# The head of a forward-and-backward kernel: skewed emission, queued loads, and w_down turned by transposing loads

## The chip, the core and the metric

The kernel runs on one core of a Trainium2 chip. The metric is device time in microseconds (us) for one execution. Five engines work side by side and meet through semaphores: PE (TensorE, matmuls and transposes into PSUM), DVE (VectorE), ACT (ScalarE), POOL (GpSimd) and SP (SyncE, which here only issues DMAs). Each engine takes its own instructions strictly in order, and so does each DMA queue. What waits at the front of a queue holds everything behind it.

## The reference

A block of a conditioned network is computed forward, and then the gradients of its output with respect to eight inputs. Cut to what matters (S = 2048 tokens, D = 576, F = 4608, bfloat16 inputs):

```python
mod = (silu(c) @ w_mod).reshape(1, 6, 1, D)            # sa, ca, ga, sb, cb, gb
h = layernorm(x) * (1 + ca) + sa
y = irfft2(rfft2(h) * (w_r + 1j * w_i))                # along tokens and features
x1 = x + ga * y
h2 = layernorm(x1) * (1 + cb) + sb
out = x1 + gb * (((h2 @ w_gate) * (h2 @ w_up)) @ w_down)
# and the gradients with respect to x, w_r, w_i, w_gate, w_up, w_down, c, w_mod, for a given grad_out
```

## The kernel before

The Fourier transforms are matmuls with tables of cosines and sines. The 2048 tokens stand as 16 tiles of 128 (token index `16 p + t`), the 289 frequencies of the feature axis as 73 groups of four. The program has three parts: the **head** (forward transform, filter, inverse transform, second normalisation, and the first backward product), the **main loop** over 36 blocks of 128 columns of F, and the **tail** (backward transform, remaining gradients, output). The change is in the head; the word "late head" is used below for its last stretch.

The head is written as plain loops, one after the other:

- **Modulation.** `mod_load(j)` brings a 576x576 piece of `w_mod` into `wm`, `mod_make(j, wm)` multiplies it (line 219, PSUM tile `modps`) and stores the result `modh[j]` to HBM from POOL's queue (line 224). Three are made ahead of stage 1, the other three after it.
- **Stage 1**, 16 steps (lines 250 to 280), one per token tile: normalise (`n`, `nm`, `hpp`), five TensorE transposes (`trp`), evacuation `hT` on ACT, column transform of ten matmuls (`zp` with the table `T_RD`), evacuation `zt`, row transform of four matmuls (`vp` with `T_G`), evacuation into `VA`.
- **Stage 2**, 19 steps (lines 292 to 332), one per 16 frequencies: transposes of `VA` (`trv`), evacuation `VT` on ACT, four matmuls with `T_BD` (`xp`), evacuation `Xc` (half on ACT, half on DVE) and its store to `xn_d`, six DVE products with the filter `wn` (`fm`, `Yg`), transposes (`try_`), `YT` on DVE, four matmuls with `T_BDA` (`ap_`), two evacuations on ACT back into `VA`.
- **Stage 3**, 16 steps (lines 341 to 384): inverse row transform (`upa`, `upb`, evacuated to `ut`), inverse column transform (`yp`, evacuated to `yb`); every second step the residual `x`, second normalisation and `h2p`, every fourth step a transposing DMA of `h2p` into `h2T`.
- **The first backward product** (lines 387 to 417), called the `ghh` work here: `grad_out` times `gb` is transposed on PE into `goT` (line 392). Then, for 18 pairs of 128-row blocks of `w_down`: a load of the pair (`wdn`), ten TensorE transposes (line 405), evacuations into `wdT` (576 on the partitions in five pieces, the fifth 64 wide), 40 matmuls (line 415, 20 per block) with `wdT` as weights, evacuations into `ghh_st` on ACT and DVE in turn, and per block a 512 KB store to `ghhT_d`.

A scheduler sets the final order: it takes the instructions by their place in the source where they are ready by its own estimate, and fills the engines with later ones where they are not. So the `ghh` work, last in the source of the head, is spread over stages 1 to 3, and what is left of it follows stage 3. PSUM of the head: five banks (`fps`) for stages 1 to 3, three (`u4ps`) for the `ghh` work. All loads and most stores are issued by SP and stand in one queue; `mod_make`'s stores, the stores of `n`, `y`, `x1` and part of the main loop's DMAs go through POOL. `wdT` and `wdn` have two buffers, each holding a pair of blocks.

The main loop (lines 462 to 516) begins with `gup` (line 492), which needs all of `h2T`, and goes on with `u8p` (lines 508 and 509) and `u57p` (line 445).

Of the kernel before, what the change touches and what calls it, by code (L numbers as in the profile page):

```python
# [10 lines left out]
BF = mybir.dt.bfloat16  # L11
# [8 lines left out]
NT = 16  # L20
S = 2048
D = 576
# [56 lines left out]
def build(ctx, tc, A_x, A_w_r, A_w_i, B_w_gate, B_w_up, B_w_down, c_in, w_mod, grad_out,  # L79
# [81 lines left out]
    with ExitStack() as hs:  # L161
# [52 lines left out]
        def mod_make(j, wm):  # L214
            for h in range(2):
                ps = fps.tile([128, 512], FP32, name="modps", tag="fp")
                for m in range(5):
                    K = KD[m]
                    nc.tensor.matmul(ps[:, 0:288], lhsT=sc_rep[0:K, m, :], rhs=wm[0:K, m, h * 288:(h + 1) * 288], start=(m == 0), stop=(m == 4))
# [24 lines left out]
        x_load(2)  # L244
        T["BD2"] = load_table(hp1, "BD2")
        T["BDA"] = load_table(hp1, "BDA")
# [3 lines left out]
        for t in range(NT):  # L250
            c4, tt = t // 4, t % 4
            if tt == 0:
                if c4 == 1:
                    x_load(3)
                xt = xts[c4]
                n1 = hw2.tile([128, 4, D], BF, name="n1")
                nmr1 = norm_stats(xt, hw2, 4, "ln1", rstd1g[:, t:t + 4])
            nc.scalar.activation(out=n1[:, tt, :], in_=xt[:, tt, :], func=ACT.Identity, bias=nmr1[:, tt:tt + 1], scale=rstd1g[:, t:t + 1])
# [9 lines left out]
            hT = hw2.tile([128, 5, 128], BF, name="hT")  # L268
            evac(hT[:], pt[:], eng="a")
            zt = hw2.tile([128, 2, FP], BF, name="zt")  # L270
            for cc in range(2):
                zp = fps.tile([128, 512], FP32, name="zp", tag="fp")
                for m in range(5):
                    nc.tensor.matmul(zp[:, :FP], lhsT=hT[:, m, :], rhs=T["RD"][:, m, cc, :], start=(m == 0), stop=(m == 4))
                evac(zt[:, cc, :], zp[:, :FP], eng=("a" if cc == 0 else "v"))
            for cc in range(2):
# [4 lines left out]

        nc.gpsimd.memset(wn[:, :, :, DF:FP], 0.0)
        nc.sync.dma_start(wn[:, 0, :, 0:DF], wr_v)
        nc.sync.dma_start(wn[:, 1, :, 0:DF], wi_v)
        for j in (MGA, MSB, MCB):
            mod_make(j, mod_load(j))
        r1.close()
        with ExitStack() as rc:  # L290
            c2 = pool("hc2", 2, "right", stack=rc)
            for ci in range(NCH):
                g0 = 4 * ci
                ng = min(4, NG - g0)
                f0, w = 4 * g0, 4 * ng
# [3 lines left out]
                VT = c2.tile([128, 4, 128], BF, name="VT")  # L299
                evac(VT[:, 0:ng, :], pt[:, 0:ng, :], eng="a")  # L300
                xp = fps.tile([128, 4, 128], FP32, name="xp", tag="fp")
                for j in range(ng):
                    nc.tensor.matmul(xp[:, j, :], lhsT=VT[:, j, :], rhs=T["BD2"][:], start=True, stop=True)
# [13 lines left out]
                Yg = c2.tile([128, 4, 128], BF, name="Yg")  # L317
# [3 lines left out]
                nc.vector.tensor_tensor(out=Ygv[:, :, :, 1, :], in0=mv_[:, 2], in1=mv_[:, 3], op=ADD)  # L321
                pt2 = fps.tile([128, 4, 128], BF, name="try_", tag="fp")
                for j in range(ng):
                    nc.tensor.transpose(pt2[:, j, :], Yg[:, j, :], ident[:])
                YT = c2.tile([128, 4, 128], BF, name="YT")
                evac(YT[:, 0:ng, :], pt2[:, 0:ng, :], eng="v")
                ap_ = fps.tile([128, 4, 128], FP32, name="ap_", tag="fp")
                for j in range(ng):
                    nc.tensor.matmul(ap_[:, j, :], lhsT=YT[:, j, :], rhs=T["BDA"][:], start=True, stop=True)
# [11 lines left out]
        for sa in range(NT):  # L341
            if sa % 2 == 0:
                xc = hw2.tile([128, 2, D], BF, name="xc")
                nc.sync.dma_start(xc[:], x_v[:, sa:sa + 2, :])
                x1 = hw2.tile([128, 2, D], BF, name="x1")
                yb = hw2.tile([128, 2, D], BF, name="yb")
                n2 = hw2.tile([128, 2, D], BF, name="n2")
            ut = hw2.tile([128, 3, 256], BF, name="ut", bufs=3)
# [9 lines left out]
            evac(ut[0:36, 2, :], upb[0:36, 0, :], eng="v")  # L358
            for h in range(2):
# [8 lines left out]
            if sa % 2 == 1:  # L368
                s0 = sa - 1
                nc.gpsimd.dma_start(y_d[:, s0:s0 + 2, :], yb[:])  # L370
                for i in range(2):
                    nc.vector.tensor_tensor(out=x1[:, i, :], in0=yb[:, i, :], in1=modh[MGA][:], op=MUL)
                    nc.vector.tensor_tensor(out=x1[:, i, :], in0=x1[:, i, :], in1=xc[:, i, :], op=ADD)
                nc.gpsimd.dma_start(x1_d[:, s0:s0 + 2, :], x1[:])
                nmr2 = norm_stats(x1, hw2, 2, "ln2", rstd2g[:, s0:s0 + 2])
                for i in range(2):
                    nc.scalar.activation(out=n2[:, i, :], in_=x1[:, i, :], func=ACT.Identity, bias=nmr2[:, i:i + 1], scale=rstd2g[:, s0 + i:s0 + i + 1])
                    nm = hw2.tile([128, D], BF, name="nm")
                    nc.vector.tensor_tensor(out=nm[:], in0=n2[:, i, :], in1=modh[MCB][:], op=MUL)
                    nc.vector.tensor_tensor(out=h2p[:, s0 + i, 0:D], in0=nm[:], in1=modh[MSB][:], op=ADD)  # L380
                nc.gpsimd.dma_start(n2_d[:, s0:s0 + 2, :], n2[:])
                if sa % 4 == 3:
                    s0 = sa - 3
                    nc.sync.dma_start_transpose(out=h2T[:, s0:s0 + 4, :, :].rearrange("q t m p -> q (t m) p"), in_=h2p[:, s0:s0 + 4, :].rearrange("p t d -> p (t d)"))
# [11 lines left out]
        for fb0 in range(0, NFB, FB4):  # L396
            nfb = min(FB4, NFB - fb0)
# [10 lines left out]
            for j in range(nfb):  # L408
                fb = fb0 + j
                st = u4w.tile([128, NT, 128], BF, name="ghh_st")  # L410
# [8 lines left out]
    with ExitStack() as ms:  # L419
# [3 lines left out]
        with ExitStack() as bs:  # L423
            FBW = 2
            FBT = 4
            wp = bs.enter_context(tc.tile_pool(name="wp", bufs=2))
            wtp = bs.enter_context(tc.tile_pool(name="wtp", bufs=2))
            ghp = bs.enter_context(tc.tile_pool(name="ghp", bufs=2))
            tp = bs.enter_context(tc.tile_pool(name="tp", bufs=2))
            tp2 = bs.enter_context(tc.tile_pool(name="tp2", bufs=2))  # L430
            sfp = bs.enter_context(tc.tile_pool(name="sfp", bufs=2))
            stg = bs.enter_context(tc.tile_pool(name="stg", bufs=4))
            wot = bs.enter_context(tc.tile_pool(name="wot", bufs=3))
            gups = bs.enter_context(tc.tile_pool(name="gups", bufs=3, space=PSUM))
            u8ps = bs.enter_context(tc.tile_pool(name="u8ps", bufs=3, space=PSUM))
            u57ps = bs.enter_context(tc.tile_pool(name="u57ps", bufs=2, space=PSUM))
# [450 lines left out]
```

## Time and profile before

| | |
|---|---|
| time, three runs | 1861.98 us median (1861.71 to 1865.2) |
| the profiled execution | 1858.56 us, of which the span of instructions is 1856.8 us |
| TensorE clock granted, mean over the span | 0.963 |
| busy: PE, DVE, ACT, POOL | 91%, 59%, 35%, 11% of the span |
| stage 1 begins (first `zp`) | 31.48 us |
| stage 2 begins (first `trv`) | 102.63 us |
| stage 3 begins (first `upa`) | 237.87 us |
| stage 3's last `yp`, late head begins | 298.93 us |
| first `u8p`: the main loop runs | 420.70 us |
| main loop gives way to the tail | about 1490 us |

The shares of the whole span are means over parts with different limits, so they are to be read stage by stage. Times are those of one profiled execution, counted from the start of its span. PE's busy time includes modelled ends of matmuls: two matmuls that follow each other closely overlap in it, and a stage in which PE is "85% busy" can still have gaps. For DMAs, SP's rows show how long the issue held the queue; "to landing" is from the issue to the semaphore that says the data is there.

### The profile page before, as it was taken

How to read it: one execution, taken by the hardware profiler on the slowest of the kernel's cores; microseconds unless marked ns; L12 is line 12 of the kernel's file. 1: busy time of each engine (PE TensorE's matmuls, PEld its weight loads, DVE VectorE, ACT ScalarE, POOL GpSimd, SP SyncE). 2: the span in 40 equal slices, each digit the busy share in tenths (PEclk: the TensorE clock that was granted, in tenths of full speed). 3: DMA queues.
4: the chain of work that ended last, by engine and by line, in shares of the span. 5: the costliest groups of instructions: out<-in, count | busy, mean ns of one | idle time of the engine just before them, and what ended most of it. 6: DMA issues, size and time to landing. Idle time of an engine off the chain costs nothing. (4 is left out here: it accounts for less than half of the span.)

```text
span 1856.8 us, 31164 instructions
## 1 busy us (share of the span) xinstructions
PE 1691.3 (91%) x11704; PEld 1059.7 (57%) x11704; DVE 1089.7 (59%) x2839; ACT 653.2 (35%) x1299; POOL 213.2 (11%) x281
## 2 busy tenths in 40 slices
PE   4988898899999999999999999999999847997895
PEld 2633343236666666666666666676666624674463
DVE  6544465127474655647465564746556489696972
ACT  4656564122222223232222223222222244333531
POOL 1000012001100101010110101011000065001320
PEclk7999999899999999999999999999999968998997
DMA  9142259527656474664747557475644565647552
GB/s 336 49 161 91 87 163 218 156 92 136 131 107 146 103 148 108 131 140 92 165 80 159 115 111 150 88 153 109 135 97 92 122 224 192 229 141 209 173 195 63
DMA packets 410537, 259.87 MB, mean 140 GB/s; under 512 B 332593, under 2 KB 380337, under 8 KB 407569
## 3 DMA queue, kind: packets, MB, share of 16 engines
q1 hardware_dynamic: 391568, 190.23, 42.6%
q0 software_dynamic: 18816, 67.65, 12.7%
q8 instruction: 91, 1.49, 0.3%
q14 instruction: 62, 0.50, 0.1%
HBM read 108.04 MB, written 79.91 MB: 101 GB/s over the span
## 5 line engine op out<-in xcount | busy, mean ns | idle before, releaser
L514 DVE TENSOR_TENSOR acc<-acc,u8p 128x288 f32<-128x288 f32 x1120 | 447.0, 450 | 402.4 <-PE u8p L509 401.3
L492 PE MATMUL gup<-h2T,wgu 128*128 128x512 bf16 x1440 | 429.2, 381 | 12.7 <-DMA wgu<-in_B_w_gate_dram 9.3
L508 PE MATMUL u8p<-wT,ggT 128*128 128x288 bf16 x1152 | 315.4, 286 | 0.0
L509 PE MATMUL u8p<-wT,guT 128*128 128x288 bf16 x1152 | 315.1, 286 | 0.0
L415 PE MATMUL u4p<-goT,wdT 128*128 128x512 bf16 (+1 forms) x720 | 204.4, 395 | 7.4 <-ACT ghh_st L130 5.5
L492 PEld LDWEIGHTS <-wgu 128*128 128x128 bf16 x1440 | 140.7, 98 | 114.2 <-issue 15.6
L446 ACT CAST so<-u57p 128x288 bf16<-128x288 f32 x216 | 86.2, 399 | 329.0 <-PE u57p L445 329.0
L509 PEld LDWEIGHTS <-guT 128*128 128x128 bf16 x1152 | 112.6, 98 | 88.3
L805 PE MATMUL u3p<-wdr,hl 128*128 128x288 bf16 x1152 | 158.4, 287 | 0.8 <-DMA hl<-hhT_d 0.8
L493 ACT CAST gT<-gup 128x512 bf16<-128x512 f32 x144 | 84.4, 586 | 201.0 <-PE gup L492 196.9
L493 ACT CAST uT<-gup 128x512 bf16<-128x512 f32 x144 | 84.4, 586 | 191.5 <-PE gup L492 116.4
L445 PE MATMUL u57p<-gon,hh_sf 128*128 128x288 bf16 x1152 | 151.3, 286 | 0.0
L445 PE MATMUL u57p<-h2p,gu_sf 128*128 128x288 bf16 x1152 | 147.4, 286 | 0.0
L445 PE MATMUL u57p<-h2p,gg_sf 128*128 128x288 bf16 x1152 | 147.2, 286 | 0.0
L445 PEld LDWEIGHTS <-hh_sf 128*128 128x128 bf16 x1152 | 112.7, 98 | 34.9
L415 PEld LDWEIGHTS <-wdT 128*128 128x128 bf16 (+1 forms) x720 | 59.8, 98 | 125.0 <-issue 91.7
L445 PEld LDWEIGHTS <-gg_sf 128*128 128x128 bf16 x1152 | 112.7, 98 | 28.4
L508 PEld LDWEIGHTS <-ggT 128*128 128x128 bf16 x1152 | 112.6, 98 | 28.4
L445 PEld LDWEIGHTS <-gu_sf 128*128 128x128 bf16 x1152 | 109.7, 98 | 29.1
L805 PEld LDWEIGHTS <-hl 128*128 128x128 bf16 x1152 | 107.8, 98 | 31.7 <-issue 3.5
L497 POOL DMA_DIRECT2D hhT_d<-hhT x36 | 33.3, 924 | 636.1 <-DVE hhT L494 524.7
L132 DVE CAST ghh_st<-u4p 128x512 bf16<-128x512 f32 x72 | 49.3, 684 | 85.9 <-PE u4p L415 71.5
(382 smaller groups left out, 1934.9 us busy)
## 6 DMA issues: line engine op xcount, KB each, us to landing
ghhT_d<-ghh_st SPq DMA_DIRECT2D x36, 512.0 KB, 3.3
ghh<-ghhT_d POOLq DMA_DIRECT2D x36, 512.0 KB, 7.5
hhT_d<-hhT POOLq DMA_DIRECT2D x36, 512.0 KB, 6.6
hl<-hhT_d SPq DMA_DIRECT2D x16, 1152.0 KB, 5.6
out_dram<-woT SPq DMA_DIRECT2D x72, 128.0 KB, 2.1
wdn<-in_B_w_down_dram SPq DMA_DIRECT2D x18, 288.0 KB, 3.2
out_dram<-so SPq DMA_DIRECT2D x36, 144.0 KB, 2.5
wdr<-in_B_w_down_dram SPq DMA_DIRECT2D x4, 1296.0 KB, 6.6
```

What stands on the lines that cost most here:

```text
L132: nc.vector.tensor_copy(dst, src)
L415: nc.tensor.matmul(pt[:], lhsT=wdT[0:K, m, j * 128:(j + 1) * 128], rhs=goT[0:K, 4 * sb4:4 * sb4 + 4, m, :], start=(m == 0), stop=(m == 4))
L445: nc.tensor.matmul(pw[:, 0:288], lhsT=sf[:, t, :], rhs=rhs_n[:, t, h * 288:(h + 1) * 288], start=(t == 0), stop=(t == NT - 1))
L446: nc.scalar.copy(so[:, h * 288:(h + 1) * 288], pw[:, 0:288])
L492: nc.tensor.matmul(pt[:], lhsT=wgu[:, wi_, m, jw * 128:(jw + 1) * 128], rhs=h2T[:, ts_, m, :], start=(m == 0), stop=(m == 4))
L493: nc.scalar.copy(dstT[:, ts_, :], pt[:])
L497: nc.gpsimd.dma_start(hhT_d[:, :, fb, :].rearrange("tp f x -> f tp x"), hhT[:].rearrange("f (tp ti) p -> f tp (ti p)", ti=2))
L508: nc.tensor.matmul(pu[:, 0:288], lhsT=ggT[:, t, :], rhs=wT[:, 0, jt, h * 288:(h + 1) * 288], start=True, stop=False)
L509: nc.tensor.matmul(pu[:, 0:288], lhsT=guT[:, t, :], rhs=wT[:, 1, jt, h * 288:(h + 1) * 288], start=False, stop=True)
L514: nc.vector.tensor_tensor(out=dst, in0=dst, in1=pu[:, 0:288], op=ADD)
L805: nc.tensor.matmul(p2[:, 0:288], lhsT=hls[fb // (NFB // 2)][:, fb % (NFB // 2), ti * 128:(ti + 1) * 128], rhs=wdr[:, fb, h * 288:(h + 1) * ...
```

## The change

Stages 1, 2 and 3 are cut into steps that a helper emits skewed: in round k, the last step of iteration k-n comes first and the first step of iteration k last. The order of the source, and with it what the scheduler prefers, is thus that of a software pipeline. `mod_make`'s store moves from POOL to SP, and its first one is named `first`; loads in `issue_after(first)` blocks are kept behind that store in SP's queue. The load, the transposes and the evacuations of `w_down` are replaced by loads that transpose. `ghh_st` gets three buffers, and the main loop's pools hand over their space tile by tile instead of pool by pool.

```diff
+    def pipeline(n, steps):
+        for k in range(n + len(steps) - 1):
+            for s_ in reversed(range(len(steps))):
+                if 0 <= k - s_ < n:
+                    steps[s_](k - s_)
...
-            nc.gpsimd.dma_start(modb_d[:, j, :], modh[j][:])
+            return nc.sync.dma_start(modb_d[:, j, :], modh[j][:]).ins
...
-        x_load(1)
-        mod_make(MSA, wms[MSA])
+        first = mod_make(MSA, wms[MSA])
         mod_make(MCA, wms[MCA])
-        nc.sync.dma_start(gon[:], go_v)
-        wms[MGB] = mod_load(MGB)
+        with tc.issue_after(first):
+            x_load(1)
+            wms[MGB] = mod_load(MGB)
+            nc.sync.dma_start(gon[:], go_v)
+            x_load(2)
+            T["BD2"] = load_table(hp1, "BD2")
+            T["BDA"] = load_table(hp1, "BDA")
         mod_make(MGB, wms[MGB])
...
+        pipeline(NT, [s1_norm, s1_cols, s1_rows])
...
+            pipeline(NCH, [s2_turn, s2_filter, s2_back, s2_inv])
...
+        pipeline(NT, [s3_rows, s3_cols, s3_norm])
...
-            wdn = u4w.tile([128, FB4, D], BF, name="wdn")
-            nc.sync.dma_start(wdn[:, 0:nfb, :], B_w_down[fb0 * 128:(fb0 + nfb) * 128, :].rearrange("(j f) d -> f j d", f=128))
-            for j in range(nfb):
-                ptw = u4ps.tile([128, 5, 128], BF, name="u4p")
-                for m in range(5):
-                    K = KD[m]
-                    nc.tensor.transpose(ptw[0:K, m, :], wdn[:, j, m * 128:m * 128 + K], ident[:])
-                evac(wdT[:, 0:4, j * 128:(j + 1) * 128], ptw[:, 0:4, :])
-                evac(wdT[0:64, 4, j * 128:(j + 1) * 128], ptw[0:64, 4, :])
+            with tc.issue_after(first):
+                for j in range(FB4):
+                    r0 = (fb0 + j) * 128
+                    nc.sync.dma_start_transpose(out=wdT[:, 0:4, j * 128:(j + 1) * 128], in_=B_w_down[r0:r0 + 128, 0:512])
+                    nc.sync.dma_start_transpose(out=wdT[0:64, 4, j * 128:(j + 1) * 128], in_=B_w_down[r0:r0 + 128, 512:576])
...
-                st = u4w.tile([128, NT, 128], BF, name="ghh_st")
+                st = u4w.tile([128, NT, 128], BF, name="ghh_st", bufs=3)
...
-            wp = bs.enter_context(tc.tile_pool(name="wp", bufs=2))
+            wp = bs.enter_context(tc.tile_pool(name="wp", bufs=2, reuse_waits="tile"))
```

What this does to the order of instructions is shown at three places. (Lines of the changed kernel are numbered anew: the matmuls of line 415 are line 457 there, `gup` is line 534, and the two new loads are lines 448 and 449.)

The first is ACT in the middle of stage 2, about one and a half steps. `trv`, `xp`, `ap_` are the PSUM tiles named above, `u4p` that of the `ghh` work. Before:

```order
L130 COPY VT<-trv 128x512
L130 CAST ghh_st<-u4p 128x512
L130 CAST Xc<-xp 128x4x16x4
L130 COPY wdT<-u4p 128x4x128 x2
L130 CAST VA<-ap__1051 128x4x16x4 x2
L130 COPY VT<-trv 128x512
```

And in the changed kernel, where the number in `ap_` shows whose step it is:

```order
L130 COPY VT<-trv 128x512
L130 CAST VA<-ap__1044 128x4x16x4 x2
L130 CAST ghh_st<-u4p 128x512
L130 CAST Xc<-xp 128x4x16x4
L130 COPY VT<-trv 128x512
```

Before, the two `VA` copies of a step stand behind its own `VT` and `Xc`, and the next `VT` behind them. Now the copies between one `VT` and the next are of an earlier step; there is at most one evacuation of `ghh` work between two `VT`, and no `wdT` copy.

The second is SP's queue in stage 2, where `xn_d` is the store of each step and `ghhT_d` that of each finished block. Before, one load per pair of blocks:

```order
L309 DMA xn_d<-Xc 128x512
L417 DMA ghhT_d<-ghh_st 128x2048
L309 DMA xn_d<-Xc 128x512
L400 DMA wdn<-in_B_w_down_dram 128x2x576
L417 DMA ghhT_d<-ghh_st 128x2048
```

In the changed kernel, two loads per block:

```order
L337 DMA xn_d<-Xc 128x512 x2
L459 DMA ghhT_d<-ghh_st 128x2048
L337 DMA xn_d<-Xc 128x512 x2
L448 DMA_TRANSPOSE wdT<-in_B_w_down_dram 128x4x128
L449 DMA wdT<-in_B_w_down_dram 64x128x1
L459 DMA ghhT_d<-ghh_st 128x2048
```

The load of the four 128-wide pieces (line 448) is a transposing DMA. That of the 64-wide piece (line 449) stands there as an ordinary DMA of shape 64x128x1: its last dimension, the run of neighbouring elements that it copies, has one element.

The third is PE in the late head. Before, a few matmuls of the main loop's first block (`gup`) stand between each pair's last transposes of `w_down` and the pair's matmuls:

```order
L405 LDWEIGHTS wdn
L405 MATMUL u4p<-ident,wdn 64x128
L492 LDWEIGHTS wgu
L492 MATMUL gup<-h2T,wgu 128x512
L492 LDWEIGHTS wgu
L492 MATMUL gup<-h2T,wgu 128x512
L415 LDWEIGHTS wdT
L415 MATMUL u4p<-goT,wdT 128x512
```

In the changed kernel the first `gup` comes when the last matmul of the `ghh` work is through:

```order
L457 LDWEIGHTS wdT
L457 MATMUL u4p<-goT,wdT 128x512
L534 LDWEIGHTS wgu
L534 MATMUL gup<-h2T,wgu 128x512
L534 LDWEIGHTS wgu
L534 MATMUL gup<-h2T,wgu 128x512
```

So all that is left of the `ghh` work now stands in one row ahead of the main loop. Of the 720 matmuls of line 415, before 60 stood ahead of stage 2, 300 within it, 56 within stage 3 and 304 after it. Of those of line 457 it is 3, 157, 61 and 499. From the first `gup` on, PE, ACT, DVE and POOL have the same instructions in the same order in both kernels.

More of the change, by code (lines that the diff above doesn't have):

```diff
@@ L253, in build @@
                 if c4 == 1:
[L254 to L258, printed above, removed]
+                    with tc.issue_after(first):
+                        x_load(3)
+                n1s[c4] = hw2.tile([128, 4, D], BF, name="n1")
+                n1s["nmr"] = norm_stats(xts[c4], hw2, 4, "ln1", rstd1g[:, t:t + 4])
+            n1 = n1s[c4]
+            nc.scalar.activation(out=n1[:, tt, :], in_=xts[c4][:, tt, :], func=ACT.Identity, bias=n1s["nmr"][:, tt:tt + 1], scale=rstd1g[:, t:t + 1])
             nm = hw2.tile([128, D], BF, name="nm")
@@ L280, in build @@
                 evac(Vv[:, :, t, cc, :], vp[:, :FP].rearrange("k (g f) -> k g f", f=4), eng=("a" if cc == 0 else "v"))
+        pipeline(NT, [s1_norm, s1_cols, s1_rows])
         nc.gpsimd.memset(wn[:, :, :, DF:FP], 0.0)
-        nc.sync.dma_start(wn[:, 0, :, 0:DF], wr_v)
-        nc.sync.dma_start(wn[:, 1, :, 0:DF], wi_v)
+        with tc.issue_after(first):
+            nc.sync.dma_start(wn[:, 0, :, 0:DF], wr_v)
+            nc.sync.dma_start(wn[:, 1, :, 0:DF], wi_v)
+            for j in (MGA, MSB, MCB):
+                wms[j] = mod_load(j)
         for j in (MGA, MSB, MCB):
-            mod_make(j, mod_load(j))
+            mod_make(j, wms[j])
         r1.close()
@@ L291, in build, with dims, s2_turn @@
             c2 = pool("hc2", 2, "right", stack=rc)
[L292 to L295, printed above, removed]
+            VTs, Ygs, YTs = {}, {}, {}
+            def dims(ci):
+                ng = min(4, NG - 4 * ci)
+                return 4 * ci, ng, 16 * ci, 4 * ng
+            def s2_turn(ci):
+                g0, ng, f0, w = dims(ci)
                 pt = fps.tile([128, 4, 128], BF, name="trv", tag="fp")
@@ L340, in build, with s3_rows @@
         Av = VA[:].rearrange("k (f c a) -> k f c a", c=2, a=NT)
[L341 to L348, printed above, removed]
+        uts, ybs = {}, {}
+        def s3_rows(sa):
+            ut = uts[sa] = hw2.tile([128, 3, 256], BF, name="ut", bufs=3)
             upa = fps.tile([128, 2, 256], FP32, name="upa", tag="fp")
@@ L358, in build, with s3_cols @@
             evac(ut[0:36, 2, :], upb[0:36, 0, :], eng="v")
+        def s3_cols(sa):
+            ut = uts[sa]
+            if sa % 2 == 0:
+                ybs[sa // 2] = hw2.tile([128, 2, D], BF, name="yb")
+            yb = ybs[sa // 2]
             for h in range(2):
@@ L367, in build @@
                 evac(yb[:, sa % 2, h * 288:(h + 1) * 288], yp[:, 0:288], eng="a")
[L368 to L384, printed above, removed]
@@ new lines, in s3_norm @@
+        def s3_norm(sa):
+            if sa % 2 == 0:
+                return
+            s0 = sa - 1
+            yb = ybs[sa // 2]
+            xc = hw2.tile([128, 2, D], BF, name="xc")
+            nc.sync.dma_start(xc[:], x_v[:, s0:s0 + 2, :])
+            x1 = hw2.tile([128, 2, D], BF, name="x1")
+            n2 = hw2.tile([128, 2, D], BF, name="n2")
+            nc.gpsimd.dma_start(y_d[:, s0:s0 + 2, :], yb[:])
+            for i in range(2):
+                nc.vector.tensor_tensor(out=x1[:, i, :], in0=yb[:, i, :], in1=modh[MGA][:], op=MUL)
+                nc.vector.tensor_tensor(out=x1[:, i, :], in0=x1[:, i, :], in1=xc[:, i, :], op=ADD)
+            nc.gpsimd.dma_start(x1_d[:, s0:s0 + 2, :], x1[:])
+            nmr2 = norm_stats(x1, hw2, 2, "ln2", rstd2g[:, s0:s0 + 2])
+            for i in range(2):
+                nc.scalar.activation(out=n2[:, i, :], in_=x1[:, i, :], func=ACT.Identity, bias=nmr2[:, i:i + 1], scale=rstd2g[:, s0 + i:s0 + i + 1])
+                nm = hw2.tile([128, D], BF, name="nm")
+                nc.vector.tensor_tensor(out=nm[:], in0=n2[:, i, :], in1=modh[MCB][:], op=MUL)
+                nc.vector.tensor_tensor(out=h2p[:, s0 + i, 0:D], in0=nm[:], in1=modh[MSB][:], op=ADD)
+            nc.gpsimd.dma_start(n2_d[:, s0:s0 + 2, :], n2[:])
+            if sa % 4 == 3:
+                s0 = sa - 3
+                nc.sync.dma_start_transpose(out=h2T[:, s0:s0 + 4, :, :].rearrange("q t m p -> q (t m) p"), in_=h2p[:, s0:s0 + 4, :].rearrange("p t d -> p (t d)"))
```

57 lines of the change are left out of this document (32 added, 25 removed).

## The prediction

> **What bounds the kernel now.** I read first the busy time by stage, since the shares of the whole span mix stages with different limits. The stretches are cut at the starts of stage 1, the second modulation part, stage 2, stage 3, the late head, the main loop and the tail.
>
> ```profile
> core 0: us, PE busy (x) PEld busy (x) DVE busy (x) ACT busy (x) POOL busy (x), PEclk, DMA share, GB/s
> 0.00:31.48 31.48, 8.61 (x36) 3.60 (x36) 16.78 (x64) 10.34 (x14) 4.80 (x14) 0.73 0.96 349
> 31.48:94.77 63.29, 58.56 (x448) 37.33 (x449) 40.31 (x119) 41.47 (x82) 1.07 (x2) 0.97 0.35 110
> 102.63:237.87 135.24, 108.51 (x673) 46.76 (x673) 59.56 (x198) 81.84 (x119) 1.07 (x2) 0.97 0.28 99
> 237.87:298.93 61.06, 60.84 (x356) 29.21 (x356) 46.19 (x136) 38.26 (x78) 10.84 (x20) 0.99 0.69 199
> 298.93:420.70 121.77, 102.42 (x416) 34.73 (x416) 33.39 (x73) 31.58 (x57) 6.82 (x12) 0.90 0.51 137
> 420.70:1490.00 1069.30, 1056.90 (x7522) 718.70 (x7521) 612.69 (x1581) 305.32 (x643) 84.15 (x128) 1.00 0.59 124
> ```
>
> The main loop is PE's, 1056.9 of 1069.3 us, and its order is the same after the change: I cost it at nothing. Stage 3 is PE's too. The slack is in the start, where DMA is 96% busy; in stage 2, where no engine is above 108.5 of 135.2 us and DMA is at 28%; and in the late head. What PE waits for in stage 2, and what one of its 19 steps looks like, is in the waits and in the timelines of PE, ACT and DVE:
>
> ```profile
> PE xp L303 <- ACT VT L130: 26.0, 18, 1.7
> DVE Xc L132 <- ACT Xc L130: 52.2, 19, 4.0
> ...
> 115.35 2.39 ACT L130 CAST VA<-ap__975 128x256 bf16<-128x256 f32 x2 [1.64 <-PE ap__975 L329]
> 117.25 0.92 ACT L130 COPY VT<-trv 128x512 bf16<-128x512 bf16 x1
> 118.06 0.59 ACT L130 CAST ghh_st<-u4p 128x512 bf16<-128x512 f32 x1
> 118.65 0.37 ACT L130 CAST Xc<-xp 128x256 bf16<-128x256 f32 x1
> 122.53 2.39 ACT L130 CAST VA<-ap__1013 128x256 bf16<-128x256 f32 x2 [1.21 <-PE ap__1013 L329]
> ...
> 118.22 0.40 PE L303 MATMUL xp<-T_BD,VT 128*128 128x128 bf16 x4 [1.40 <-ACT VT L130]
> 121.03 0.39 PE L324 MATMUL try__1006<-ident,Yg 128*128 128x128 bf16 x4
> 122.10 0.40 PE L329 MATMUL ap__1013<-T_BDA,YT 128*128 128x128 bf16 x4
> ...
> 119.06 0.42 DVE L132 CAST Xc<-xp 128x256 bf16<-128x256 f32 x1 [3.77 <-ACT Xc L130]
> 120.41 0.28 DVE L321 TENSOR_TENSOR Yg<-fm 128x256 bf16<-128x256 bf16 x1
> 121.45 0.42 DVE L132 COPY YT<-try__1006 128x512 bf16<-128x512 bf16 x1 [0.17 <-PE try__1006 L324]
> ```
>
> Read by start times: `VA` 115.35, `VT` 117.25, `xp` 118.22, `Xc` 118.65 and 119.06, `Yg` 120.41, `try_` 121.03, `YT` 121.45, `ap_` 122.10, next `VA` 122.53. It is one ring, 7.18 us around, through three engines, closed because the next `VT` stands behind this step's `VA` on ACT. Stage 2 is bound by latency, and matmuls of the `ghh` work fill PE meanwhile.
>
> **The change part by part.** The sum is made against the profiled execution, span 1856.8 and time 1858.56 us, which is 3.4 us under the median of the runs.
>
> *Start.* PE's first waits, with four rows that the terms below use:
>
> ```profile
> 6.94 5.07 PE L219 MATMUL modps<-wm,sc_rep 128*128 128x288 bf16 x20 [6.94 <-DVE sc_rep L206]
> 27.15 2.90 PE L219 MATMUL modps<-wm,sc_rep 128*128 128x288 bf16 x10 [15.14 <-DMA wm<-in_w_mod_dram]
> 375.22 0.60 PE L492 MATMUL gup<-h2T,wgu 128*128 128x512 bf16 x2
> 375.67 10.37 PE L415 MATMUL u4p<-goT,wdT 128*128 128x512 bf16 x40
> 0.00:420.70 420.70, 20.83 (x180) 12.76 (x180) 0.94 0.48 149
> 31.48:94.77 63.29, 14.40 (x49) 4.21 (x49) 0.97 0.35 110
> ```
>
> The second row: the third `wm` sits behind the 2304 KB of `gon` in SP's queue and holds stage 1 for 15.1 us. In the new order it comes ahead of `gon`. 2304 KB at 349 GB/s are 6.8 us, so stage 1 begins about 7 us sooner. The two modulation stores now stand in SP's queue and wait for PE (first row, to 12.0 us) and DVE; behind them stand `xt`, `wm`, `gon`, while `T_RD` and `T_G` are already on their way. If that cover failed, nothing would be gained; the other end is 12 us. POOL loses six issues that nobody waits for.
>
> *Stage 1*, 63.3 us. Of PE's 58.6 us, 14.4 are `ghh` matmuls (the last row) and about 2 transposes of `w_down`. 42 us remain, with ACT and DVE below 40. Only 3 `ghh` matmuls stay ahead of stage 2. With three steps in flight I take 48 us: 15 less (ends 0 and 21, PE's 42 without a gap).
>
> *Stage 2.* With four steps in flight the ring is open, and the fullest engine sets the pace. By start times on ACT: `VA` 1.90, `VT` 0.81, `Xc` 0.37 and 0.8 of a `ghh_st` at 0.59 make 3.6 us a step. PE has 16 small matmuls, 0.9 us in four groups spaced about 0.23, and 8 `ghh` matmuls at 0.26: 3.0. I take 3.9 us; 19 steps and 5 us to fill the pipeline are 79, 56 us less than 135. Ends: 65 less (3.6 us, short fill) and 25 less (5.5 us, if `fps`' five banks or the one `fm` buffer couple the steps).
>
> *Stage 3* has 61 instead of 56 `ghh` matmuls and is PE's already: nothing, ends 4 less, 6 more.
>
> *The transposes* on PE (line 405, 20.8 us in all, the last row but one above) go, with 72 evacuations. This is not a term of its own: those in stages 1 and 2 are already counted, and some 8 of them, 9 us, lie in the late head, where the next term counts the new content afresh.
>
> *Late head.* Here the postponed matmuls arrive: 499 instead of 304. At 10.37 us per 40 they are 129 us; with 40 `gup` at 0.22 (from 375.22 to 375.67 for two) the main loop begins 138 us after stage 3, against 121.8: 16 more, if the loads keep up. Then the whole sum is -7 -15 -56 +16 = -62. Whether they do hangs on the second load, line 449: 64x128x1, so 8192 runs of two bytes. The only relatives in the trace are `c_bf`, 128x4x1, and the store `gcf` of the same form. The DMA counts of two windows around them, the issues of transposing loads, and the issue of two loads of 2048 runs each:
>
> ```profile
> DMA packets 650, 0.13 MB, mean 193 GB/s; under 512 B 564, under 2 KB 640, under 8 KB 650
> ...
> q1 hardware_dynamic: 535, 0.00, 36.3%
> ...
> L477 SPq DMA_TRANSPOSE wT<-in_B_w_gate_dram x45: 1217/1258/4692, 315.6 to 1237.6; - x45
> ...
> L665 SPq DMA_DIRECT2D wn<-in_A_w_r_dram x1: 384/384/384, 1579.0 to 1579.0; - x1
> L666 SPq DMA_DIRECT2D wn<-in_A_w_i_dram x1: 7610/7610/7610, 1579.5 to 1579.5; - x1
> ```
>
> The first is 4.0 to 4.7 us, around `c_bf`: 564 tiny packets in 0.70 us, mixed with others, 1.24 ns each over 16 engines. The second (packets, MB, share of 16 engines) is 1843.9 to 1844.6 us, around `gcf`, alone: 535 packets took 36.3% of 16 engines for 0.70 us, 7.6 ns of one engine each. The last two rows show that a load of many runs holds SP's queue: the second issue took 7.61 us. So line 449 costs 8192 x 7.6 / 16 = 3.9 us when all engines are kept full. It costs 10.2 us at the rate around `c_bf`. I take 3.9, the row with nothing else in it; a value between, 5.6 us, is the same `gcf` burst if its 512 runs are set against the half of the window that they fill.
>
> The queue then carries per block: 3.9, the transposing load of 512 packets (about 0.6 of engine time; its issue of 1.26 us lies beside line 449 draining), and the 512 KB store, 1.5 us at 349 GB/s: 6.0 us against 5.2 of PE. About 20 blocks are still to be loaded, since `wdT` holds two pairs: 120 us. To this come 20 `wT` issues at 1.26 us, 25 us; 15 us at the beginning, in which SP waits for a pair to come free (59 matmuls of the blocks in hand at 0.26); the last pair's 10 us on PE; and `gup`'s 9. That is 179 us, 57 more than 121.8.
>
> The sum: -7 -15 -56 +57 = **-21 us**, 1837.6 us for the execution and about 1841 on the scale of the median. I say 1840.
>
> A rule of the Trainium skill speaks against this change. Its page "VectorE: DVE Perf Modes", section "The three transpose paths", gives 1309 ns for a DMA transpose of 128x128 and 390 ns on TensorE, and warns that a plain DMA that transposes by strides is 19 times slower than the transposing one. For half such a tile that would be an estimate of 12.4 us in place of 3.9, which puts 20 x 8.5 = 170 us more on the sum. Line 449 falls under it: the page "DMA: Bandwidth & Descriptors", section "DMA Transpose (X-bar)", says that a DRAM input with a free dimension below 128 is moved by a rearranged access pattern instead. No run here has such a load of that size.
>
> **The rivals.** *The loads hide.* If line 449 takes 3 us or less (runs overlapping in an engine), the late head is PE's, 138 us: 1797 to 1815. The 7.6 ns speak against it.
>
> *The element loads become the bound, slower than before.* Place: SP's queue in the late head. The sum is zero where line 449 costs 3.9 + 21/20 = 5.0 us. Up to 8 us it costs 20 x 3 more than that, to 1920 and, once stage 2's eleven loads (11 x 10.8 = 119 us instead of 79) hold it as well, 1960. At 10.2 us: 20 x 6.3 + 60 - 21 = +165, or 2025. For it speaks that the loads read HBM in two-byte pieces, which the `gcf` row does not; against it that `c_bf` shared the engines. The page's rule above is this rival at its far end.
>
> *The skew does not open the ring.* At 5.5 us a step, stage 2 gives 25 instead of 56: +10, so 1870. The scheduler's order, which does put an earlier step's `VA` between two `VT`, speaks against it.
>
> **How the numbers follow.** Forecast, line 449 between 3 and 5 us: 0.40, 1822 to 1858. Loads hidden: 0.12. Loads bound, 5 to 8 us: 0.20, 1862 to 1960; above 8 us: 0.17. Ring not opened: 0.11. Runs of this kernel differ by up to 0.2% (1861.71 to 1865.2), so within 3.7 us nothing can be told. Faster takes the hidden case, nearly all of the forecast and a little of the last: 0.51. The same takes 0.09 from the edges of forecast, bound loads and ring. Slower is the rest: 0.40. The range leaves out the slowest loads, 0.17, and the lowest end: 1803 to 1960.
>
> **What would show it.** Right: stage 1 begins near 24 us; stage 2 lasts 75 to 85 us with ACT above 85% busy; no wait of `xp` for `VT`; PE's `ghh` matmuls of the late head wait for DMA into `wdT`, some 40 us in total; packets below 512 B rise by 36 x 8192. Wrong: SP rows of line 449 of 8 us or more, or `ghh` matmuls waiting for `wdT` in stage 2 already; or a late head without waits. A main loop that is not 1069 us would fell the premise that only the head changes.

## The result, and the profile after

The changed kernel takes **2035.3 us** (median of four, 2031.7 to 2038.0) against 1861.9 us before: ratio **1.0928**, 95% interval 1.0905 to 1.0951. It is 173 us slower; 1840 us was predicted, and the range ended at 1960. The profiled execution has a span of 2029.9 us (before: 1856.8).

The busy time by stage, cut at the same places as in the prediction: starts of stage 1, second modulation part, stage 2, stage 3, late head, main loop and tail. The columns are those of the prediction's first fence. Two rows of before, main loop and tail, stand last.

```profile
0.00:24.41 24.41, 9.12 (x35) 3.72 (x36) 15.86 (x61) 8.77 (x13) 2.63 (x10) 0.81 0.95 337
24.41:68.05 43.64, 42.26 (x359) 29.91 (x360) 35.96 (x108) 33.91 (x70) 1.60 (x3) 0.95 1.42 180
68.05:97.07 29.02, 9.11 (x56) 4.37 (x54) 3.96 (x12) 2.98 (x7) 0.00 (x0) 0.65 1.55 110
97.07:198.62 101.55, 69.91 (x450) 33.67 (x450) 46.91 (x168) 63.50 (x90) 0.52 (x1) 0.80 1.21 76
198.62:281.73 83.11, 70.54 (x350) 30.36 (x351) 45.53 (x131) 37.91 (x77) 11.34 (x21) 0.83 1.17 139
281.73:592.40 310.67, 197.26 (x541) 52.22 (x541) 44.91 (x80) 35.42 (x61) 6.26 (x11) 0.71 1.44 78
592.40:1661.70 1069.30, 1056.89 (x7522) 718.71 (x7521) 612.57 (x1581) 305.32 (x643) 83.73 (x128) 1.00 0.60 124
1661.70:2029.90 368.20, 288.02 (x2219) 187.11 (x2218) 276.44 (x665) 143.45 (x306) 104.14 (x102) 0.90 0.54 175
...
420.70:1490.00 1069.30, 1056.90 (x7522) 718.70 (x7521) 612.69 (x1581) 305.32 (x643) 84.15 (x128) 1.00 0.59 124
1490.00:1856.80 366.80, 287.74 (x2219) 186.10 (x2218) 276.77 (x665) 143.40 (x306) 103.31 (x102) 0.90 0.55 175
```

The main loop is 1069.30 us in both, to the hundredth. Everything happens in the head. Against before: start -7.1, stage 1 -19.7, second modulation part +21.2 (29.0 against the 7.9 us from 94.77 to 102.63), stage 2 -33.7, stage 3 +22.0, late head +188.9, tail +1.4; together +173.1. From stage 1 to the late head the DMA share is above 1 throughout, where before it was 0.96 in the start, 0.92 in the short second modulation part and at most 0.69 in the other stages of the head. (A share above 1 says that the times of packets overlap in an engine.) Packets below 512 bytes rose from 332,593 to 647,376; 36 loads of 8192 runs are 294,912 of the difference.

PE's longest waits in the head, two of its rows, and the two new loads:

```profile
PE u4p L457 <- DMA wdT<-in_B_w_down_dram: 111.2, 24, 11.1
PE modps L226 <- DMA wm<-in_w_mod_dram: 27.5, 2, 19.9
...
94.24 2.89 PE L226 MATMUL modps<-wm,sc_rep 128*128 128x288 bf16 x10 [19.91 <-DMA wm<-in_w_mod_dram]
170.63 1.49 PE L457 MATMUL u4p<-goT,wdT 128*128 128x512 bf16 x3
...
L448 SPq DMA_TRANSPOSE wdT<-in_B_w_down_dram x36: 1195/1939/12617, 38.7 to 561.3; - x36
L449 SPq DMA_DIRECT2D wdT<-in_B_w_down_dram x36: 604/622/1254, 40.1 to 563.3; - x36
...
wdT<-in_B_w_down_dram SPq DMA_DIRECT2D x36, 16.0 KB, 14.3
```

The issue of line 449 itself takes 0.62 us. Its data needs 14.3 us to land, and whatever comes next in SP's queue stands for most of that time. One block of the late head, from the timelines of SP (start, us of issue) and of PE, with the DMA counts of the 8.5 us that begin with the row 461.09:

```profile
458.40 1.91 SPq L448 DMA_TRANSPOSE wdT<-in_B_w_down_dram  x1
460.36 0.62 SPq L449 DMA_DIRECT2D wdT<-in_B_w_down_dram  x1
461.09 8.61 SPq L459 DMA_DIRECT2D ghhT_d<-ghh_st  x1
469.75 1.98 SPq L448 DMA_TRANSPOSE wdT<-in_B_w_down_dram  x1
...
452.11 8.30 PE L457 MATMUL u4p<-goT,wdT 64*128 64x512 bf16 x20 [3.07 <-DMA wdT<-in_B_w_down_dram]
...
GB/s 58 96 308 308 154 308 308 0 308 34 120 176 276 16 5 5 5 4 3 3 2 2 2 2 2 2 2 2 2 2 2 2 2 2 2 2 2 2 2 2
DMA packets 7446, 0.54 MB, mean 63 GB/s; under 512 B 7350, under 2 KB 7350, under 8 KB 7446
q1 hardware_dynamic: 7446, 0.54, 158.3%
```

The store at 461.09 is held for 8.61 us. It does not wait for its data: it is the 24th store, and the evacuations of the 24th block ended at 448.2 us. The block's cycle is 469.75 - 458.40 = 11.35 us, and SP's rows fill it without a gap. PE's 20 matmuls would need 5.2 us of it at 0.26 us each; here they take 8.30 after a wait of 3.07. In the GB/s row the large packets of an earlier store are gone after a third of the window; the rest is two-byte runs at 2 GB/s, about one per ns over all engines. 7350 small packets in 8.5 us are **1.16 ns each, 9.5 us for the 8192 of one load**.

### The profile page after: what moved, and what is told of

Same layout as the page of the kernel before. It is cut to its first block, busy times and chain, and to the rows that moved or that the text cites. A ratio compares the mean times of both kernels' runs of the same rounds, so it can differ in the third digit from the quotient of the medians.

```text
span 2029.9 us, 30799 instructions
## 1 busy us (share of the span) xinstructions
PE 1743.1 (86%) x11524; PEld 1060.0 (52%) x11524; DVE 1082.1 (53%) x2803; ACT 631.3 (31%) x1263; POOL 210.2 (10%) x275
## 2 busy tenths in 40 slices
DMA packets 721286, 259.85 MB, mean 128 GB/s; under 512 B 647376, under 2 KB 691280, under 8 KB 718320
## 5 line engine op out<-in xcount | busy, mean ns | idle before, releaser
L457 PE MATMUL u4p<-goT,wdT 128*128 128x512 bf16 (+1 forms) x720 | 263.2, 489 | 113.4 <-DMA wdT<-in_B_w_down_dram 111.2
L457 PEld LDWEIGHTS <-wdT 128*128 128x128 bf16 (+1 forms) x720 | 67.8, 111 | 289.3 <-issue 150.3
L130 ACT CAST ghh_st<-u4p 128x512 bf16<-128x512 f32 x72 | 45.5, 634 | 271.8 <-PE u4p L457 198.4
```

The source lines that it names most:

```text
L130: nc.scalar.copy(dst, src)
L457: nc.tensor.matmul(pt[:], lhsT=wdT[0:K, m, j * 128:(j + 1) * 128], rhs=goT[0:K, 4 * sb4:4 * sb4 + 4, m, :], start=(m == 0), stop=(m == 4))
```

## The experiments

The runs below test three theories of the loss. **Theory A:** the two-byte runs of line 449 are the whole loss. **B:** turning `w_down` by DMA costs SP's queue its time in any form. **C:** the skewed order does the harm. Each run had its own runs of the kernel before on the same chip (medians 1863.6 to 1866.7 us); ratios are against those.

*As many bytes, in 64 runs of 256 bytes* (e1_contig). It leaves out the turning of the fifth piece.

```diff
-  nc.sync.dma_start_transpose(out=wdT[0:64, 4, j*128:(j+1)*128], in_=B_w_down[r0:r0+128, 512:576])
+  nc.sync.dma_start(wdT[0:64, 4, j*128:(j+1)*128], B_w_down[r0:r0+64, 448:576])
```

> The changed kernel, with the load of the 64-wide fifth piece (line 449) replaced by a plain load of the same 16 KB in 64 runs of 256 bytes; the fifth piece of wdT then holds untransposed numbers, so that part of the product is not the reference's. Theory A, the two-byte runs are the whole loss: SP's queue no longer stands 7 to 12 us behind each of these loads, the late head is PE's again (about 140 us instead of 310), the gap of 20 us ahead of stage 2 is gone, and the time is 1795 to 1830 us. Theory B, turning w_down by DMA costs the queue its time in either form: the other transposing load and the store still take 11 us per block, 1960 us or more. Theory C, the skewed order does the harm (gaps and a lower granted clock in stages 2 and 3): 1860 us or more, with the late head mended and the stages not.

Measured 1796.2 us, ratio 0.962 (0.9584 to 0.9656), at the lower end of what theory A gave. Its windows, from the start to the late head, and then the tail:

```profile
0.00:24.80 24.80, 9.34 (x36) 3.76 (x37) 15.88 (x61) 8.79 (x13) 2.63 (x10) 1.00 0.94 337
24.80:68.88 44.08, 42.70 (x358) 30.14 (x359) 36.02 (x108) 33.89 (x70) 1.60 (x3) 1.00 0.63 180
68.88:76.70 7.82, 7.82 (x56) 4.12 (x53) 3.96 (x12) 2.99 (x7) 0.00 (x0) 1.00 0.92 317
76.70:140.70 64.00, 59.38 (x451) 28.66 (x451) 46.44 (x168) 61.79 (x90) 0.53 (x1) 1.00 0.38 128
140.70:202.64 61.94, 61.02 (x350) 28.66 (x351) 47.91 (x137) 38.24 (x78) 11.01 (x21) 1.00 0.70 198
202.64:353.10 150.46, 143.15 (x541) 44.76 (x541) 42.94 (x75) 35.51 (x61) 6.61 (x12) 0.95 0.53 157
...
1422.40:1796.80 374.40, 294.92 (x2219) 189.06 (x2218) 276.71 (x665) 143.67 (x306) 103.39 (x102) 0.88 0.55 172
```

Nothing in the program but the form of one 16 KB load is different, and the gap ahead of stage 2, the slow stages 2 and 3 and 160 us of the late head are gone. Theory A holds, B and C fall: the skewed order is all here, and its stages are fast.

*The reference computed with 128-wide loads* (e2_wide): columns 448 to 575 are turned, and the repeated 64 rows meet zeros.

```diff
-  in_=B_w_down[r0:r0+128, 512:576]   # into wdT[0:64, 4, ...]
+  in_=B_w_down[r0:r0+128, 448:576]   # into wdT[:, 4, ...]
+  nc.gpsimd.memset(goT[0:64, :, 4, :], 0.0)
+  evac(goT[64:128, t, 4, :], pt[64:128, 4, :])      # pt piece 4: gon columns 448:576
-  matmul(pt, lhsT=wdT[0:K, m, ...], rhs=goT[0:K, ...])
+  matmul(pt, lhsT=wdT[:, m, ...], rhs=goT[:, ...])
```

> The changed kernel, with the fifth piece loaded as a full 128-wide transposing load of columns 448 to 575; its first 64 rows repeat piece four and meet zeros in goT. Theory A: as in the run with the plain load, plus one more transposing issue per block, 36 x 1.2 us of SP's queue, which PE's 5.2 us per block cover: 1795 to 1835 us. Theory B: two transposing loads of 1.9 us and a store per block still outlast PE, 1960 us or more. Theory C: 1860 us or more.

Measured **1786.1 us**, ratio 0.9564 (0.9542 to 0.9586): it beats both kernels, is the fastest measured here, and lies 9 us below the expectation. The loads in its trace, and for comparison the 290 matmuls without a gap in the late head of e1_contig and of this kernel:

```profile
L450 SPq DMA_TRANSPOSE wdT<-in_B_w_down_dram x36: 1189/1257/3058, 39.2 to 317.8; - x36
L451 SPq DMA_TRANSPOSE wdT<-in_B_w_down_dram x36: 1211/1243/2411, 40.6 to 319.7; - x36
...
269.69 74.79 PE L457 MATMUL u4p<-goT,wdT 128*128 128x512 bf16 x290
...
269.74 62.76 PE L458 MATMUL u4p<-goT,wdT 128*128 128x512 bf16 x290
```

At 64 columns the transposing call of line 449 became a plain `DMA_DIRECT2D`; at 128 it is a `DMA_TRANSPOSE` of 1.24 us. The two last rows show something that no theory had: 0.258 us a matmul with a 64-row one in every five, 0.216 us with all at 128 rows. Over the 499 `ghh` matmuls of the late head that is some 21 us; the late head is 9.2 us shorter than in e1_contig (141.3 against 150.5), since PE waits more in it (17.7 against 7.3 us).

*The skew and the queued loads alone* (e3_pe), with the old w_down path, and *the loads alone* (e4_loads), with the old order. Their edits are the two halves of the diff above; e3_pe has `ghh_st` with two buffers.

> The changed kernel with the old path of w_down (one plain load per pair, ten TensorE transposes, evacuations; ghh_st with two buffers for want of space): the skew and the queued loads alone. Theories A and B: PE gets its 21 us of transposes back, mostly in stages that it does not fill, so about 15 us more than the 128-wide loads, 1805 to 1840 us. Theory C: 1860 us or more, since the skewed order is all there.

> The kernel before with nothing changed but the w_down path: the two loads of lines 448 and 449 in place of the load, transposes and evacuations. Theory A: 36 loads hold the queue 11 us each; stages 1 to 3 cover some of it, the late head is SP's at 11.4 us per block and 1.5 to 2 times its 122 us: 1920 to 2030 us. Theory B: the same. Theory C: within 20 us of the kernel before, 1842 to 1882 us.

e3_pe: 1822.2 us, 0.9762 (0.9732 to 0.9793). e4_loads: 2030.2 us, 1.0873 (1.0833 to 1.0912). So the skew with its queued loads gains 2.4% with the old path, and the element loads lose 8.7% without any skew. With them the skew gains nothing: 2030 without it, 2035 with it. Theory A's numbers held, at the upper edge for e4_loads; theory C's was missed by 150 us.

*128-wide loads without the skew* (e7_wideonly).

> The kernel before, with the w_down path alone exchanged for transposing loads that are 128 wide throughout; no skew, no queued loads. Stages keep their 135 and 61 us. Theory A, the two halves of the change gain separately: late head without the transposes on PE and its waits for wdT evacuations, with matmuls of 0.216 instead of 0.259 us (62.76 us for 290 against 74.79 us): 304 x 0.043 = 13 and some 9 us less: 1815 to 1845 us. Rival, the loads gain only in company of the skew: within 8 us of before. Rival, they are most of the gain: below 1805 us.

1833.2 us, 0.9822 (0.9799 to 0.9846), as theory A had it. The skew gives 2.4%, the wide loads 1.8%, and both together 4.4%. How much of the 1.8% is due to full rows alone is the question of e10_pad, below.

*Half the runs* (e6_fourbyte). This, too, leaves out the turning of the fifth piece.

```diff
+  nc.sync.dma_start(wdT[0:64, 4, j*128:(j+1)*128].rearrange("p (r c) -> p r c", c=2),
+                    B_w_down[r0:r0+64, 448:576].rearrange("r (p c) -> p r c", c=2))
```

> The changed kernel, with line 449 bringing the same 16 KB in 4096 runs of four bytes in place of 8192 of two (the fifth piece of wdT then holds wrong numbers, so that part of the product is not the reference's). Theory runs: the price is per run; about 5 us a load, the break-even of the prediction. Against the run with 64 long runs (1796 us): 20 blocks of the late head at 6.9 instead of 5.2 us give 34 more, stage 2 about 12 more: 1825 to 1865 us. Theory bytes, or a fixed cost of such a load: nothing changes, 2020 to 2045 us.

1813.8 us, 0.9728 (0.9708 to 0.9747): below both expectations. The timeline of SP in its late head, and the GB/s of one of its blocks, 307.3 to 311.9 us:

```profile
307.39 1.33 SPq L448 DMA_TRANSPOSE wdT<-in_B_w_down_dram  x1
308.76 0.62 SPq L450 DMA_DIRECT2D wdT<-in_B_w_down_dram  x1
309.49 2.25 SPq L460 DMA_DIRECT2D ghhT_d<-ghh_st  x1
...
GB/s 11 9 7 7 185 359 534 392 285 392 534 285 392 392 249 249 285 65 161 278 285 256 121 11 0 1 1 0 2 4 9 10 11 11 11 11 11 11 11 11
```

The store is held 2.25 instead of 8.61 us, and the cycle of a block, about 4.5 us, is below PE's 5.2. Alone in the engines four-byte runs move at 11 GB/s, so 0.36 ns each; two-byte runs need about 1 to 1.16. A load of 4096 four-byte runs is some 1.5 us, a sixth of 8192 two-byte runs. So the price is neither per run nor per byte; why two bytes are so much dearer, no run here shows. The 18 us above e1_contig lie in the late head (169.1 against 150.5 us), where PE waits 23.1 instead of 7.3 us.

*Every second element load from ACT's queue* (e5_twoqueues).

> The changed kernel, with the load of line 449 of every second block issued by ACT, so into another queue. Theory engines: the 16 DMA engines work through two-byte runs at 1.16 ns each whichever queue they come from (7350 small packets in 8.5 us in the late head of the changed kernel); the loads of a pair can overlap, but not faster: 1990 to 2045 us. Theory queue: one queue takes runs at that rate and two take them twice as fast; the cycle of a block falls from 11.4 to about 6 us and the time to 1840 to 1920 us. If ACT is held by its own issues, stage 2 shows it in ACT's rows.

2057.5 us in a single run (before: 1864.6), 12 us above the range of the theory of the engines and far outside that of the theory of the queue. The DMA issues in 420 to 600 us:

```profile
DMA packets 134164, 11.27 MB, mean 63 GB/s; under 512 B 131984, under 2 KB 131984, under 8 KB 134160
wdT<-in_B_w_down_dram ACTq DMA_DIRECT2D x7, 16.0 KB, 27.0
wdT<-in_B_w_down_dram SPq DMA_DIRECT2D x7, 16.0 KB, 24.5
```

And the packets of the changed kernel in 411.4 to 570 us:

```profile
DMA packets 122804, 9.76 MB, mean 62 GB/s; under 512 B 121010, under 2 KB 121010, under 8 KB 122802
```

131984 small packets in 180 us are 1.36 ns each, 121010 in 158.6 us are 1.31: no gain from a second queue, and a load now lands after 24.5 to 27.0 us instead of 14.3. The engines set the rate, not SP's queue. The Trainium skill says so too, in "DMA: Bandwidth & Descriptors", section "Rules for kernel authors": spreading DMAs over issuing engines does not help, since all run on the same 16 DMA engines.

*Stage 2 without its skew* (e8_s2plain): e2_wide with the four steps called one after the other for each `ci`.

> The kernel with 128-wide loads (1786 us), with stage 2's four steps emitted one after the other again, stages 1 and 3 skewed as before. Theory ring: a step is 7 us again and stage 2 about 135 instead of 63 us, 72 more; about 140 more ghh matmuls find room in it and leave the late head, 31 less: 1815 to 1840 us. Rival, the scheduler opens the ring by itself once the transposes and their evacuations are gone from PE and ACT: 1780 to 1795 us.

1805.3 us, 0.969 (0.9671 to 0.9708), below the expected range. Stage 2 and late head here, then the same two of e2_wide:

```profile
75.80:206.70 130.90, 101.27 (x660) 48.74 (x660) 60.24 (x189) 77.75 (x111) 0.53 (x1) 1.00 0.36 118
265.90:360.10 94.20, 77.34 (x329) 32.66 (x330) 28.50 (x55) 22.91 (x40) 6.75 (x12) 0.91 0.63 177
...
76.10:139.40 63.30, 53.94 (x450) 29.34 (x450) 46.15 (x168) 61.55 (x90) 0.53 (x1) 1.00 0.39 132
199.73:341.00 141.27, 123.58 (x541) 53.87 (x541) 43.10 (x76) 35.22 (x61) 6.82 (x12) 0.93 0.59 171
```

The ring is real: 130.9 against 63.3 us. But of the 67.6 us that opening it gains, the late head takes 47.1 back. Of the `ghh` matmuls that fill PE inside the ring in e8_s2plain, some 210 (541 less 329 instructions) stand there in e2_wide, at 0.22 us each. The expectation had counted 140 of them.

*Zero rows to 128 in the kernel before* (e10_pad).

```diff
+  nc.gpsimd.memset(goT[64:128, :, 4, :], 0.0)
+  nc.gpsimd.memset(wdT[64:128, 4, :], 0.0)
-  matmul(pt, lhsT=wdT[0:K, m, ...], rhs=goT[0:K, ...])
+  matmul(pt, lhsT=wdT[:, m, ...], rhs=goT[:, ...])
```

> The kernel before with one thing changed: the fifth piece of goT and of wdT is filled with zeros to 128 rows, so that all ghh matmuls contract over 128. Theory A: 0.21 us less per group of five; 61 groups lie in the late head and 11 in stage 3, both PE's: 15 us less, 1844 to 1853 us against 1863. Rival, the late head waits for evacuations of wdT and not for PE: within 4 us of before.

1837.8 us, 0.986 (0.9835 to 0.9885): 1.4% for two memsets and a slice, nearly double the expected gain.

```profile
367.41 8.80 PE L416 MATMUL u4p<-goT,wdT 128*128 128x512 bf16 x40
```

40 matmuls take 8.80 instead of 10.37 us. So full rows alone give 1.4 of the 1.8% that e7_wideonly gave. That would leave about 0.4% for turning `w_down` by DMA instead of TensorE without the skew; it is a difference of two runs, hardly larger than their intervals, and neither shows it alone. Late head 108.7 against 121.8 us and stage 3 59.0 against 61.1 are as worked out; stage 2 gave another 8 (127.1 against 135.2), which the expectation had left out.

*Full rows in stage 3* (e9_best), *stores on POOL* (e11_poolstore), *both* (e12_padpool), all from e2_wide: `yp` contracts over 128 rows of a zeroed `ut` for its third piece; `ghhT_d` is stored by `nc.gpsimd` instead of `nc.sync`.

> The kernel with 128-wide loads (1786 us), with stage 3's column transform on all 128 rows: the third piece of ut has 36 valid rows, and is now read whole, its other rows zeroed once. Theory A, a matmul with fewer rows costs the switch: as with the ghh matmuls, where four full and one 64-row matmul take 0.0415 x 5 = 0.21 us more than five full ones, here about 0.2 us for each of 32 groups, 6 us, of a stage that PE bounds: 1776 to 1783 us. Rival, it is a property of the 64-row form or hidden: 1784 to 1788 us.

> The kernel with 128-wide loads (1786 us), with the ghhT_d stores issued by POOL instead of SP. Theory queue order: in the late head PE waits 17.7 us, 11.3 for ACT, which waits for a ghhT_d store that stands in SP's queue behind h2T's transposing load and ten wT loads; from POOL's queue, idle there, the stores go at once: 10 to 15 us less, 1771 to 1778 us. Rival, the next thing is late in their place (wdT loads still stand behind the wT loads: 6.4 us of PE's waits now): 1780 to 1787 us.

> The kernel with 128-wide loads and full-row yp matmuls (1795 us), with the ghhT_d stores issued by POOL. Theory queue order: the 4 us that stage 3 gained were lost because one store, held 18 us behind h2T's load, stopped ACT and then PE for 15.3 us; with the stores on POOL that wait goes, and the gain of stage 3 shows: 3 to 6 us below the run with POOL stores alone, 1765 to 1775 us. Rival, the loss has another cause: it stays above the run with POOL stores alone.

1795.1 us (ratio 0.9625, 0.9601 to 0.9649), 1788.6 (0.9604, 0.9587 to 0.9621) and 1794.1 (0.9629, 0.9613 to 0.9644): none is better than e2_wide. In e9_best stage 3 fell from 60.3 to 56.1 us as expected, but the late head grew from 141.3 to 154.7. PE's waits in the late head, e2_wide first, then e9_best, then e11_poolstore:

```profile
PE u4p L458 <- ACT ghh_st L130: 11.3, 3, 5.3
PE u4p L458 <- DMA wdT<-in_B_w_down_dram: 6.4, 3, 3.3
...
PE u4p L460 <- ACT ghh_st L130: 24.3, 3, 15.3
PE u4p L460 <- DMA wdT<-in_B_w_down_dram: 5.3, 2, 3.4
...
PE u4p L458 <- DMA wdT<-in_B_w_down_dram: 24.2, 2, 16.5
```

The 15.3 us of e9_best are in its timelines of SP and ACT:

```profile
205.35 9.20 SPq L431 DMA_TRANSPOSE h2T<-h2p  x1
214.67 0.52 SPq L462 DMA_DIRECT2D ghhT_d<-ghh_st  x1
...
230.38 1.07 ACT L130 CAST ghh_st<-u4p 128x512 bf16<-128x512 f32 x2 [18.38 <-DMA ghhT_d<-ghh_st]
```

A store whose data was ready at 204.5 us stands behind a transposing load of `h2T`, is issued at 214.67 and lands at 230.3, and so holds `ghh_st`, ACT and PE. Of ACT's 18.4 us of waiting, from 212.0 on, 2.7 lie before the issue and 15.6 are the landing: the place in the queue is the smaller part of it. With the stores on POOL that wait is gone, but PE waits 24.2 us for `wdT` loads, which then stand behind `wT` loads, where it waited 17.7 for both in e2_wide. For e11_poolstore and e12_padpool the rival's account came true (e11_poolstore lies 2 us above its rival's range). e9_best met neither of its ranges: the stage gained what theory A gave it, and the stretch behind it lost more. Why e12_padpool stays 5 us above e11_poolstore is open; its PE waits 26.1 us for `wdT`.

## Why the prediction was wrong, point by point

**The step that failed is one term of the late head: the price of line 449.** I took 3.9 us, from the `gcf` row at 7.6 ns of an engine per run. It measured 9.5 us by the rate, and 9.3 by the cycle (11.4 less the 0.6 and 1.5 us that the sum counted beside it). By the DMA counts above a run takes 28.9 ns of an engine (158.3% of 16 engines for 8.5 us, over 7446 packets), with 1.6 of them overlapping; the `gcf` row had 7.6 and I let none overlap. The other row I had, around `c_bf`, gave 10.2. It was a load like line 449, and `gcf` is a store. I chose the row that was clean over the row that was of the same direction, though the rival named the reading of two-byte pieces. Whether the direction makes the difference, or the 512 runs of `gcf` against 8192, no run here shows.

The estimate of 12.4 us from the Trainium skill ("VectorE: DVE Perf Modes", "The three transpose paths") was nearer than my choice too. In e2_wide a 128x128 transposing load takes 1.24 us to issue and 2.6 to land; line 449 takes 9.5 us by its rate and 14.3 to land for half the tile. That is 15 times as slow by the first pair and 11 times by the second, where that page says 19. The page says it for a large innermost stride of the destination; here it is the source that is read with a stride.

**Late head:** +57 predicted, +188.9 measured. The loads left in it:

```profile
L449 SPq DMA_DIRECT2D wdT<-in_B_w_down_dram x22: 604/622/1254, 289.6 to 563.3; - x22
```

With the term put right the rest of that sum stands: 20 blocks at 11.4 instead of 6.0 us are 108 more, and 22 loads were left instead of 20, another 23; together 131 of the 132 that are missing. Some of that agreement is luck: of the terms beside the blocks, the wait at the beginning was 8 us (289.6 less 281.7) and not 15, and what came between the cycles was 34 us (from the first to the last load 273.7, less 21 cycles of 11.4) and not the 25 of the `wT` issues.

**Start, -7:** right, -7.1, and for the reason given: PE's wait for the third `wm` fell from 15.1 to 7.6 us. **Stage 1, -15:** 43.6 us against 48 predicted, so -19.7, but the 20 us came back at once in the second modulation part: its last `wm` stood in SP's queue behind four element loads. I had asked who waits behind line 449 only in the late head and in stage 2. This is a second step that failed: the second modulation part and stage 3, both put at nothing, lost 43 us together.

**Stage 2, -56:** -33.7 in the changed kernel, -71 without the element loads (64.0 us in e1_contig), more than the better end of 65. The ring opened as said: ACT is busy 61.8 of 64.0 us, 3.4 us a step where I worked out 3.6 and took 3.9. With the element loads a step has to wait for its stores instead. ACT's waits in stage 2 of the changed kernel show 24.2 us of the 37.6 by which it is longer than in e1_contig:

```profile
ACT Xc L130 <- DMA xn_d<-Xc: 24.2, 5, 7.5
```

**Stage 3, nothing:** +22.0. Without the element loads it is +0.9, so these are the element loads' too; in SP's queue the loads of `x` that come next after a line 449 in this stage stand 7 to 12 us.

**The hidden-loads sum** of -62 was right as a sum: e1_contig is 60.0 us below before (1796.8 against 1856.8). That the sum is so near is luck: stage 1 and stage 2 gave 20 more, the late head took 13 more and the tail 8.

**The rivals.** "Element loads bound, above 8 us" is what happened. It was priced at 2025 and given 0.17; 2035 came. Of the signs, the start (24.4 us), the packets and the main loop came as said. PE's waits for `wdT` in the late head were 111 us and not some 40, and stage 2 lasted 101.6 us and not 75 to 85. The sign against, rows of line 449 of 8 us or more, stands one row further on in SP's queue: line 449 takes 0.62 us, and what follows it 8.6 in the block shown. The break-even of 5.0 us cannot be read off e6_fourbyte, since four-byte runs turned out far cheaper than half.

## What to carry to other kernels

A strided load of single two-byte elements cost about 1.2 ns for each run here, over all the DMA engines, and everything behind it in the queue paid most of that too; widening the tile until the transposing DMA applied, with half of it thrown away, removed the price. When two rows of a trace disagree about a price, do not take the clean one for being clean: here the mixed one, which moved in the same direction through the same kind of memory, was the nearer. At the least let both ends into the range. Before counting a stage's gain, ask what work had filled its gaps: it goes somewhere, and here 70% of what opening the ring gave came back behind it.

## What was unexpected of the hardware

- **A 64-row matmul among 128-row ones costs 0.21 us per group of five** (62.76 against 74.79 us for 290). With zero rows in their place, all five are at the 0.216 us of the others. The Trainium skill's page "TensorEngine Tiling (Array Packing)", section "Key Properties", says that a change of tiling mode drains TensorE; that would fit, but no run here shows the drain itself.
- **Two bytes are far dearer than four**: 1 to 1.16 ns a run where nothing else is in the engines, against 0.36 ns.
- **Waits seem to cost PE twice.** With 450 and 451 instructions in stage 2 PE is busy 69.9 us in the changed kernel and 59.4 in e1_contig, at a granted clock of 0.80 against 1.00; three `ghh` matmuls took 1.49 us (row 170.63) where 0.78 is usual (3 x 0.26), and after a wait of 3.07 us twenty took 8.30 instead of 5.2 (row 452.11; granted clock 0.59 in these 8.4 us). That the waits bring the clock down is how these rows look; no run here changes the waits alone.
